# Filler transposes and matmuls on TensorE in the opening of a beacon-attention and maxout-FFN kernel

## The chip, the core and the metric

The kernel runs on one core of one Trainium2 chip. The metric is the device time of one execution in microseconds. The core has TensorE (PE in the profile; its weight loads are PEld), VectorE (DVE), ScalarE (ACT), GpSimd (POOL) and SyncE (SP), and 16 DMA engines. TensorE writes to banks of PSUM; the other engines read these and write SBUF.

## What is computed

Eight batches of eight heads of attention over 576 tokens and 16 beacon keys and values in front of them; the beacons are always visible, the rest is causal. The result is laid out as 4608 tokens of 512 features and goes through a feed-forward layer with the maximum of three products.

```python
k_all = concatenate([beacon_k, k], axis=2)     # 8 x 8 x 592 x 64
v_all = concatenate([beacon_v, v], axis=2)
scores = 1 / sqrt(64) * matmul(q, k_all.transpose(0, 1, 3, 2))
scores = where(causal, -1e9, scores)           # beacons are never masked
a = softmax(scores)
x = matmul(a, v_all).transpose(0, 2, 1, 3).reshape(4608, 512)
h = maximum(maximum(x @ w1, x @ w2), x @ w3)   # 512 -> 768
out = h @ w_out                                # 768 -> 512
```

## The kernel before

Everything on the matmul side is bf16. Heads are worked on in pairs, p from 0 to 31, four pairs a batch; two pairs make a quad. For a pair, q and k must first be turned so that the 64 features lie on partitions: the tile `qT` holds both heads of a pair on 2 x 64 partitions, `kT` the same with the 16 beacons in front. For the later batches that is a transposing DMA, for the first four batches TensorE transposes (L345, L360) with `ident` and an evacuation by VectorE or ScalarE.

The scores of a pair are made in four groups of (key tile, query range) pieces (L432, `emit_scores`): TensorE writes a group of both heads into a tile `sc` of two banks, of which there are two, and ScalarE takes the exponential of the whole group into `at_sb` (L451). Pieces on the diagonal are masked by VectorE (a product with `tri`, L468) or GpSimd (L470). `emit_pv` (L490) multiplies with ones and with v into the banks `pv0` and `pv1`, or into two `fps` banks; ScalarE inverts the sums (L534, L536) and VectorE multiplies (L546) into `xT`. FFN units (L565, L586, L605) use the `fps` banks.

The order of every engine's instructions is the order of the program's text (`tc.manual_schedule()`), so TensorE works strictly through its list; a wait there holds up all behind it. The opening, batch 0, has an order written out by hand in `start` (L711) and `first_steps` (L780). `T(p, h, pv)` (L752) there turns one half (288 tokens, h = 0 or 1) of pair p, by `turn_half` (L351): six transposes for q, an evacuation, six for k, an evacuation. The sources are the tiles `quad`, loaded by GpSimd's queue in `load_quad` (L206), q before k for each. With `pv` true the banks `pv0` and `pv1` are used, else two `fps` banks of bf16. `M` masks, `V` casts a tile of v, `P` is `emit_pv`, `F(n)` emits n FFN units, and `G(p)` loads a later pair with a gate: VectorE writes one element of the stage tile first, so that the load on SyncE's queue does not start ahead of VectorE's earlier work.

`keep_busy` (L407) multiplies the constant tile `busy` (ones, 128 x 320) with itself into the bank `pv1`; nobody reads the result. It is called with 12 at the start, and with 2 ahead of the second turn:

```python
    keep_busy(12)                        # L712
    ...
    turn_half(0, 0, False, by_act)       # L736
    turn_beacons(0, 1, bk16_0)
    cast_half(1, 0, by_dve)
    cast_half(1, 1, by_dve)
    keep_busy(2)                         # L740
    turn_half(1, 0, True)
```

Of the kernel before, what the change touches and what calls it, by code (L numbers as in the profile page):

```python
# [9 lines left out]
BF16 = mybir.dt.bfloat16  # L10
# [6 lines left out]
def kernel(  # L17
# [13 lines left out]
    nc = tc.nc  # L31
# [5 lines left out]
    d_model, d_ff = moe_w1.shape  # L37
# [12 lines left out]
    HALF = S // 2  # L50
# [70 lines left out]
    ffn_psum = ctx.enter_context(tc.tile_pool(name="ffn_psum", bufs=2, space=PSUM))  # L121
# [14 lines left out]
    busy = const.tile([128, 320], BF16, name="busy")  # L136
    nc.vector.memset(busy, 1.0)
    ident = const.tile([128, 128], BF16, name="ident")
# [15 lines left out]
    def pv_bank(i, shape, dtype):  # L154
        return pv_psum.tile(shape, dtype, name=f"pv{i}")
# [34 lines left out]
    def load_half(p, i, queue):  # L190
        st = half_pool.tile([QP, 2, HR, D], FP32, name=f"h32{i}")
        queue.dma_start(
            out=st.rearrange("p h r d -> p h (r d)"),
            in_=half_source(p // PPQ, 0, i, 2 * (p % PPQ), 2),
        )
        stage["half", p, i] = st

    def cast_half(p, i, cast):
        t16 = half_pool.tile([QP, 2, HR, D], BF16, name=f"h16{i}")
        cast(  # L200
            t16.rearrange("p h r d -> p (h r d)"),
            stage.pop(("half", p, i)).rearrange("p h r d -> p (h r d)"),
        )
        stage["half16", p, 0, i] = t16

    def load_quad(g, h):  # L206
        for i in range(2):
            t16 = const.tile([QP, 4, HR, D], BF16, name=f"quad{g}{h}{i}")
            nc.gpsimd.dma_start(  # L209
                out=t16.rearrange("p h r d -> p h (r d)"), in_=half_source(g, h, i, 0, 4)  # L210
            )
            for j in range(PPQ):
                stage["half16", PPQ * g + j, h, i] = t16[:, 2 * j : 2 * j + 2]
# [78 lines left out]
    def load_beacons(b0, b1, dst, queue=None):  # L292
        for b in range(b0, b1):
            (queue or nc.sync).dma_start(
                out=dst[Nb * (b - b0) : Nb * (b - b0 + 1)],
                in_=beacon_k[b].rearrange("h n d -> n h d"),
            )

    def turn_beacons(b0, b1, src):
        n = Nb * (b1 - b0)  # L300
        ps = sc_psum.tile([128, PPB, n], BF16, name="sc")
        for pi in range(PPB):
            nc.tensor.transpose(
                ps[:, pi],
                src[:, 2 * pi : 2 * pi + 2].rearrange("p h d -> p (h d)"),
                ident[0:n, 0:n],
            )
        if b0 == 0:
            by_act(kTs[0][:, 0:Nb], ps[:, 0, 0:Nb])
        by_act(bT[:, :, Nb * b0 : Nb * b1], ps)  # L310
# [37 lines left out]
                ident[0:QP, 0:QP],  # L348
            )

    def turn_half(p, h, pv, q_copy=None):  # L351
        for i in range(2):
            src = stage.pop(("half16", p, h, i))
            if pv:
                ps = pv_bank(i, [128, 1024], BF16)[:, 0:HALF]
            else:
                ps = ffn_psum.tile([128, HALF], BF16, name="fps")
            for r in range(HR):
                for e in range(2):
                    nc.tensor.transpose(  # L360
                        ps[64 * e : 64 * e + 64, r * QP : (r + 1) * QP],
                        src[:, e, r],
                        ident[0:QP, 0:QP],
                        tile_position=(0, 64 * e),
                    )
            x0 = i * Nb + HALF * h
            dst = (qTs, kTs)[i][p % NT][:, x0 : x0 + HALF]
            (q_copy if i == 0 and q_copy else by_dve)(
                dst.rearrange("d (p r) -> d p r", r=HR), ps.rearrange("d (r p) -> d p r", r=HR)
            )  # L370
# [7 lines left out]
    def place_beacons(p, copy):  # L378
        b, pi = divmod(p, PPB)
        copy(kTs[p % NT][:, 0:Nb], bT[:, pi, Nb * b : Nb * (b + 1)])  # L380
# [26 lines left out]
    def keep_busy(n, cols=320, ffn=False):  # L407
        ps = ffn_psum.tile([128, 512], FP32, name="fps") if ffn else pv_bank(1, [128, 512], FP32)
        for _ in range(n):
            nc.tensor.matmul(  # L410
                ps[:, 0:cols], busy[:, 0:128], busy[:, 0:cols], start=True, stop=True
            )
# [270 lines left out]
    def L(fn, *a):  # L683
        return lambda: fn(*a)
# [14 lines left out]
    def next_load(n=1):  # L699
        for _ in range(n):  # L700
            if loads:
                loads.pop(0)()
# [8 lines left out]
    def start():  # L711
        keep_busy(12)  # L712
        load_half(0, 0, nc.sync)
        load_half(0, 1, nc.scalar)
        load_half(1, 0, nc.sync)
        load_beacons(0, 1, bk32_0, nc.scalar)
        load_half(1, 1, nc.scalar)
        make_identity(nc, ident)
        nc.gpsimd.memset(tri, 1.0)
        nc.gpsimd.affine_select(  # L720
            out=tri,
            in_=tri,
            compare_op=ALU.is_ge,
            fill=0.0,
            base=0,
            pattern=[[1, 128]],
            channel_multiplier=-1,
        )
        load_quad(1, 0)
        load_quad(0, 1)  # L730
        load_quad(1, 1)
        next_load(3)
        cast_half(0, 0, by_dve)
        cast_half(0, 1, by_act)
        by_dve(bk16_0, bk32_0)
        turn_half(0, 0, False, by_act)  # L736
        turn_beacons(0, 1, bk16_0)
        cast_half(1, 0, by_dve)
        cast_half(1, 1, by_dve)
        keep_busy(2)  # L740
        turn_half(1, 0, True)
        place_beacons(1, by_dve)

# [5 lines left out]
    def steps(p):  # L749
        return [[0, 1], [2, 3]]  # L750

    def T(p, h, pv, q_copy=None):  # L752
        def run():
            turn_half(p, h, pv, q_copy)
            if h == 0:
                place_beacons(p, by_dve)

        return run

    def M(p, gi, dve=False):  # L760
        return L(emit_masks, p, gi, dve)
# [4 lines left out]
    def V(t):  # L766
        return L(cast_first_v, t)
# [7 lines left out]
    def F(n):  # L775
# [2 lines left out]
    cast_p = L(by_pool, bk16_1, bk32_1)  # L778

    first_steps = [  # L780
        ((0, 0), [T(2, 0, False)]),
        ((1, 0), [M(0, 0, True), T(3, 0, True), V(0), V(1)]),
        ((2, 0), [T(0, 1, False), V(2), L(load_w, 0, 0, d_ff)]),
        ((3, 0), [T(1, 1, True), M(1, 0, True), M(2, 0, True)]),
        ((0, 1), [M(0, 1)]),
        ((0, 2), [T(2, 1, False), M(3, 0, True), M(0, 2), V(3), V(4)]),
        ((0, 3), [M(0, 3, True), L(load_w, 1, 0, d_ff)]),
# [18 lines left out]
    for b in range(2, B):  # L806
        p = b * PPB
# [6 lines left out]
    for b in range(B_PE, B):  # L814
        p = b * PPB
# [8 lines left out]

    def emit_all():
        start()
        for group, fns in first_steps:
            if group:
# [104 lines left out]
```

## Time and profile before

| | |
|---|---|
| median of 5 runs | 304.03 us (303.51 to 304.90) |
| the profiled execution, its own time | 304.90 us |
| its span, first to last instruction | 303.2 us |
| TensorE busy | 286.6 us, 95% of the span |
| VectorE, ScalarE, GpSimd busy | 177.4, 144.9, 127.8 us |
| HBM read, written | 35.13, 14.22 MB |
| chain that ended last | PE 80%, DMA 5%, SyncE's queue 5%, DVE 3% |

The profiled execution is the slowest of the five shown, 0.87 us over the median; 1.7 us of it lie outside the span. "Busy" of TensorE counts from an instruction's start to a modelled end, and matmuls overlap, so it overstates the work. The page's slices divide the span in 40 parts of 7.58 us, with a digit for the busy share in tenths; PEclk is the clock that the throttle granted to TensorE. In rows of the timeline the first number is the start in us from the span's beginning, the second the length of the group, and the bracket gives the engine's idle time before it with what ended it. A form such as 96*64 96x96 is the rows and columns of the stationary operand, then partitions and columns of the moving one.

### The profile page before, as it was taken

How to read it: one execution, taken by the hardware profiler on the slowest of the kernel's cores; microseconds unless marked ns; L12 is line 12 of the kernel's file. 1: busy time of each engine (PE TensorE's matmuls, PEld its weight loads, DVE VectorE, ACT ScalarE, POOL GpSimd, SP SyncE). 2: the span in 40 equal slices, each digit the busy share in tenths (PEclk: the TensorE clock that was granted, in tenths of full speed). 3: DMA queues.
4: the chain of work that ended last, by engine and by line, in shares of the span. 5: the costliest groups of instructions: out<-in, count | busy, mean ns of one | idle time of the engine just before them, and what ended most of it. 6: DMA issues, size and time to landing. Idle time of an engine off the chain costs nothing.

```text
span 303.2 us, 8599 instructions
## 1 busy us (share of the span) xinstructions
PE 286.6 (95%) x3542; PEld 154.2 (51%) x3572; DVE 177.4 (59%) x357; ACT 144.9 (48%) x222; POOL 127.8 (42%) x253
## 2 busy tenths in 40 slices
PE   7898987999998999999999999999999999999994
PEld 3545653555444545454545687645454544444442
DVE  3753783655766575746674666466746675274372
ACT  3665475775565465635564556455645531401300
POOL 6170668466648674466445644562243210000000
PEclk9999999999999999999999999999999999999999
DMA  9995999999989999999979999994102001103003
GB/s 153 201 170 141 205 222 236 265 200 272 265 225 262 170 307 234 184 206 284 255 174 191 280 273 177 168 239 119 43 35 106 2 0 71 71 1 134 5 2 141
DMA packets 85320, 50.68 MB, mean 167 GB/s; under 512 B 64416, under 2 KB 80032, under 8 KB 85280
## 3 DMA queue, kind: packets, MB, share of 16 engines
q1 hardware_dynamic: 80672, 45.76, 66.9%
q0 software_dynamic: 4048, 4.03, 8.0%
q8 instruction: 28, 0.46, 0.7%
q10 hardware_dynamic: 560, 0.33, 0.5%
q14 instruction: 12, 0.10, 0.1%
HBM read 35.13 MB, written 14.22 MB: 163 GB/s over the span
## 4 chain that ended last, share of the span: by engine, by line
PE 80%; DMA 5%; SPq 5%; DVE 3%; POOL 2%; issue 2%; ACT 2%; POOLq 0%; DVEq 0%
PE fps L574 30%; PE sc L574 12%; PE pv L514 12%; PE fps L610 11%; PE sc L442 8%; PE sc L610 4%; SPq L245 3%; DMA quad<-in_k_dram 3%; DMA st<-in_k_dram 2%; PE sc L345 1%; ACT at_sb L451 1%; POOL quad L209 1%; SPq L180 1%; DVE y L618 1%; PE fps L514 1%
## 5 line engine op out<-in xcount | busy, mean ns | idle before, releaser
L451 ACT ACTIVATE at_sb<-sc 128x928 bf16<-128x928 f32 (+5 forms) x128 | 104.0, 861 | 89.7 <-PE sc L442 88.6
L574 PE MATMUL fps<-xT,w_sb 128*128 128x512 bf16 (+1 forms) x464 | 106.4, 356 | 2.4 <-issue 0.8
L470 POOL TENSOR_SCALAR_AFFINE_SELECT at_sb<-at_sb 128x256 bf16<-128x256 bf16 (+2 forms) x148 | 53.8, 383 | 103.0 <-ACT at_sb L451 102.8
L574 PEld LDWEIGHTS <-w_sb 128*128 128x128 bf16 x672 | 61.7, 97 | 65.5 <-issue 12.3
L584 DVE TENSOR_TENSOR hT<-hT,fps 128x512 bf16<-128x512 bf16 x70 | 47.9, 687 | 30.2 <-PE fps L574 29.7
L218 POOL CAST p<-st 96x768 bf16<-96x768 f32 x56 | 44.6, 822 | 0.5 <-DMA st<-in_k_dram 0.4
L574 PE MATMUL sc<-xT,w_sb 128*128 128x512 bf16 (+1 forms) x187 | 42.9, 356 | 0.1
L442 PE MATMUL sc<-qT,kT 64*128 64x288 bf16 (+5 forms) x400 | 38.1, 292 | 2.8 <-ACT at_sb L451 1.2
L610 PE MATMUL fps<-w_out_sb,hT 128*128 128x512 bf16 x143 | 34.6, 379 | 0.9 <-issue 0.6
L610 PEld LDWEIGHTS <-hT 128*128 128x128 bf16 x210 | 19.8, 98 | 24.1 <-DVE hT L584 2.1
L584 DVE TENSOR_TENSOR hT<-hT,sc 128x512 bf16<-128x512 bf16 x32 | 22.0, 688 | 16.3 <-PE sc L574 10.6
L618 DVE COPY y<-fps 128x512 f32<-128x512 f32 x25 | 17.3, 691 | 22.7 <-PE fps L610 22.7
L514 PE MATMUL pv<-at_sb,v_sb 128*32 128x288 bf16 (+5 forms) x1376 | 29.6, 233 | 0.0
L442 PEld LDWEIGHTS <-kT 64*128 64x128 bf16 x400 | 14.9, 97 | 28.1 <-issue 23.1
L582 DVE CAST hT<-fps 128x512 bf16<-128x512 f32 x32 | 22.0, 690 | 12.1 <-PE fps L574 12.1
L546 DVE TENSOR_TENSOR xT<-pv,recip 128x288 bf16<-128x288 f32 (+2 forms) x93 | 27.2, 348 | 2.6 <-ACT recip L536 2.6
L514 PEld LDWEIGHTS <-v_sb 128*32 128x32 bf16 (+1 forms) x1408 | 25.0, 98 | 2.7 <-issue 0.6
L514 PE MATMUL pv<-at_sb,ones 128*32 128x288 bf16 (+4 forms) x500 | 18.6, 263 | 1.1 <-POOL at_sb L470 0.9
L261 POOL CAST v_sb<-st 128x1536 bf16<-128x1536 f32 (+2 forms) x21 | 18.4, 893 | 0.6 <-DMA st<-in_v_dram 0.6
L534 ACT ACTIVATE lnd<-pv 128x288 f32<-128x288 f32 x31 | 12.9, 416 | 8.2 <-PE pv L514 8.1
L514 PEld LDWEIGHTS <-ones 128*32 128x32 bf16 (+2 forms) x512 | 11.2, 97 | 9.6 <-issue 6.6
L582 ACT CAST hT<-sc 128x512 bf16<-128x512 f32 x6 | 3.5, 586 | 23.7 <-PE sc L574 23.7
(70 smaller groups left out, 165.1 us busy)
## 6 DMA issues: line engine op xcount, KB each, us to landing
out_dram<-y SPq DMA_DIRECT2D x35, 256.0 KB, 3.1
st<-in_q_dram SPq DMA_DIRECT2D x28, 288.0 KB, 5.3
st<-in_k_dram SPq DMA_DIRECT2D x28, 288.0 KB, 5.7
st<-in_v_dram SPq DMA_DIRECT2D x24, 256.0 KB, 5.9
w_sb<-in_moe_w_dram POOLq DMA_DIRECT2D x6, 384.0 KB, 6.7
q_dram<-p SPq DMA_DIRECT2D x16, 144.0 KB, 2.4
k_dram<-p SPq DMA_DIRECT2D x16, 144.0 KB, 2.7
st<-in_v_dram SPq DMA_DIRECT2D x8, 224.0 KB, 6.2
```

Source lines behind the costliest of these rows:

```text
L218: cast(t16.rearrange("p r h d -> p h r d"), st[0:QP, i * NQ2 : (i + 1) * NQ2].rearrange("p (h r d) -> p h r d", h=2, r=QR),)
L261: cast(v_sb[0:n, t:t1].rearrange("p t h d -> p (t h d)"), st[0:n, (t - t_lo) * H * D : (t1 - t_lo) * H * D],)
L442: nc.tensor.matmul(ps[:, e, off : off + q1 - q0], kT[hs, 128 * t : 128 * t + 128], qT[hs, q0:q1], start=True, stop=True, tile_position=(64 ...
L451: nc.scalar.activation(out=both_heads(p, gi), in_=ps[:, :, 0 : g_width(p, gi)], func=AF.Exp, scale=scale)
L470: nc.gpsimd.affine_select(out=view, in_=view, compare_op=ALU.is_ge, fill=0.0, base=x0, pattern=[[0, 2], [1, hi - lo]], channel_multiplier=-1,)
L514: nc.tensor.matmul(ps[bank][32 * j : 32 * j + 32, lo + q0 - qa : lo + qb - qa], lhsT, at_view(PPQ * quad + j // 2, t, j % 2, q0, qb), star ...
L546: nc.vector.tensor_mul(xT[:, 2 * g + part - 1, c0 + ca : c0 + cb], ps[bank][:, lo : lo + cb - ca], recip[:, ca:cb],)
L574: nc.tensor.matmul(ps[:, o0 : o0 + n], w_in[i][:, ct, 128 * ft : 128 * (ft + 1)], xT[:, ct, x0 : x0 + n], start=(ct == 0), stop=(ct == n_c ...
L582: (by_act if alone[0] else by_dve)(h, ps)
L584: nc.vector.tensor_max(h, h, ps)
L610: nc.tensor.matmul(ps, hT[:, ft, 128 * tt : 128 * (tt + 1)], w_out_sb[:, ft, :], start=(ft == 0), stop=(ft == n_ft - 1),)
L618: nc.vector.tensor_copy(y, ps)
```

## The change

`turn_half` gets an argument `idle`. Ahead of the k transposes of a turn it now puts that many transposes of `busy` by `ident`, 128 x 128 each, into columns 512 to 1023 of the bank that the k transposes are about to write in columns 0 to 287; nobody reads these columns. Four turns of `first_steps` get six each. The `fps` tile of a turn is now 1024 columns of bf16, a whole bank. After the very first turn `keep_busy(3)` is added. TensorE's list grows by 27 weight loads and 27 matmuls or transposes; the lists of the other engines and the DMAs stay as they were.

```diff
+    def fill(ps, n):
+        for i in range(n):
+            x0 = 512 + 128 * (i % 4)
+            nc.tensor.transpose(ps[:, x0 : x0 + 128], busy[:, 0:128], ident)
+
-    def turn_half(p, h, pv, q_copy=None):
+    def turn_half(p, h, pv, q_copy=None, idle=0):
         for i in range(2):
             src = stage.pop(("half16", p, h, i))
             if pv:
-                ps = pv_bank(i, [128, 1024], BF16)[:, 0:HALF]
+                bank = pv_bank(i, [128, 1024], BF16)
             else:
-                ps = ffn_psum.tile([128, HALF], BF16, name="fps")
+                bank = ffn_psum.tile([128, 1024], BF16, name="fps")
+            ps = bank[:, 0:HALF]
+
+            fill(bank, idle if i == 1 else 0)
             for r in range(HR):
...
         turn_half(0, 0, False, by_act)
+        keep_busy(3)
         turn_beacons(0, 1, bk16_0)
...
-    def T(p, h, pv, q_copy=None):
+    def T(p, h, pv, q_copy=None, idle=0):
         def run():
-            turn_half(p, h, pv, q_copy)
+            turn_half(p, h, pv, q_copy, idle)
...
-        ((0, 0), [T(2, 0, False)]),
-        ((1, 0), [M(0, 0, True), T(3, 0, True), V(0), V(1)]),
-        ((2, 0), [T(0, 1, False), V(2), L(load_w, 0, 0, d_ff)]),
-        ((3, 0), [T(1, 1, True), M(1, 0, True), M(2, 0, True)]),
+        ((0, 0), [T(2, 0, False, None, 6)]),
+        ((1, 0), [M(0, 0, True), T(3, 0, True, None, 6), V(0), V(1)]),
+        ((2, 0), [T(0, 1, False, None, 6), V(2), L(load_w, 0, 0, d_ff)]),
+        ((3, 0), [T(1, 1, True, None, 6), M(1, 0, True), M(2, 0, True)]),
```

## The prediction

> **What bounds the kernel now.** I read the slice rows of the page first, then the chain of waits over the first 40 us, then TensorE's timeline of the opening, and last ScalarE's.
>
> ```profile
> PE   7898987999998999999999999999999999999994
> PEclk9999999999999999999999999999999999999999
> DMA  9995999999989999999979999994102001103003
> ```
>
> A slice is 7.58 us. From the eighth slice on TensorE is full to the end but for one digit, so whatever is won or lost before about 50 us is carried to the end unless something else paces the stretch between. PEclk says full clock everywhere, even in the first slices, and that is where this page misleads: the matmuls themselves say otherwise.
>
> ```profile
> 1.32 3.38 PE L410 MATMUL pv<-busy 128*128 128x320 bf16 x12 [1.32 <-DVE busy L137]
> ...
> 8.37 0.45 PE L360 MATMUL fps<-ident,quad 96*64 96x96 bf16 x6
> 9.11 0.45 PE L360 MATMUL fps<-ident,quad 96*64 96x96 bf16 x6 [0.29 <-DMA quad<-in_k_dram]
> 9.49 0.61 PE L442 MATMUL sc<-qT,kT 64*128 64x288 bf16 x6
> 10.03 0.69 PE L360 MATMUL pv<-ident,quad 96*64 96x96 bf16 x12
> 10.66 0.61 PE L442 MATMUL sc<-qT,kT 64*128 64x288 bf16 x6
> 11.19 0.45 PE L360 MATMUL fps<-ident,quad 96*64 96x96 bf16 x6
> 12.01 0.45 PE L360 MATMUL fps<-ident,quad 96*64 96x96 bf16 x6 [0.37 <-DMA quad<-in_k_dram]
> 12.40 0.61 PE L442 MATMUL sc<-qT,kT 64*128 64x288 bf16 x6
> 12.93 0.69 PE L360 MATMUL pv<-ident,quad 96*64 96x96 bf16 x12
> ...
> 25.95 1.74 PE L593 MATMUL fps<-xT,w_sb 128*128 128x256 bf16 x8
> ...
> 28.56 1.05 PE L593 MATMUL fps<-xT,w_sb 128*128 128x256 bf16 x8
> ```
>
> The columns are start, length, engine, line, instruction, count, and the idle time before with what ended it. The last two lines are the same eight matmuls: 1.74 us at 25.95, 1.05 us at 28.56. With the 0.28 us tail of the last one taken off, the seven gaps are 0.21 us and 0.11 us. The twelve dummies at the top start 0.267 us apart, 0.83 ns a column; the later rate is half that. So **the gate is shut from the first instruction to about 27.4 us** (the starts of single instructions change pace at 27.4, where the trace's clock record also begins; the page takes the time before it for full). Even transposes obey it: the 96-column ones of L360 take 281 ns, those of L345 at 35 us take 206 ns.
>
> Before about 15 us TensorE works in its fixed order behind the quarter loads:
>
> ```profile
> 5.36 9.73 DMA quad<-in_k_dram
> 15.09 0.04 issue
> 15.13 0.45 PE fps L360 x6
> 15.58 0.94 PE sc L442 x6
> 16.52 2.00 PE pv L514 x37
> ```
>
> This is the chain of waits. After 15.1 it is TensorE almost without a break (pv, sc, fps, pv, fps) to 27.7, interrupted by one ScalarE exponential at 22.5, then by the one at 28.05, and at 29.4 it goes through the gated pair loads into SyncE's queue and the transfers, until a cast at 50.3. Beside it runs ScalarE:
>
> ```profile
> 13.05 4.50 ACT L451 ACTIVATE at_sb<-sc 128x1024 bf16<-128x1024 f32 x5 [0.72 <-PE sc L442]
> 18.98 0.78 ACT L451 ACTIVATE at_sb<-sc 128x736 bf16<-128x736 f32 x1 [1.43 <-PE sc L442]
> ```
>
> Five exponentials back to back from 13.05 to 17.55. With two score buffers, the scores of the fifth of these wait for the third exponential. A delay ahead of 13.05 therefore reaches the first big pv stretch at 16.45 through ScalarE, however early the last load lands.
>
> **The change, part by part.** Nothing is removed or moved, no DMA is added, and every queue but TensorE's keeps its order. The waits on a bank's earlier user pass from the k transposes to the fills ahead of them; a fill waits for a bank, never for the load behind it. What is added is 3 matmuls of 320 columns and 24 transposes of 128 columns.
>
> *The three dummies after the first turn.* The first turn issues its last transpose at 5.22, and the beacon transposes wait for a VectorE cast until 6.37 (0.86 us idle in the row of L303). Three times 0.267 us is 0.80 us: 5.35 to 6.15. Cost nothing, covered by that cast; if the cast were earlier, up to 0.8 us.
>
> *The fills at the shut clock.* Six times 128 columns at 0.83 ns is 0.64 us each. The trace has no such transpose. Below: with the clock open, half, 0.32 us. Above: if the 128-column weight loads did not overlap, another 0.10 us each (the weight loads of L410 last 102 to 152 ns, yet its matmuls start exactly 320 columns apart, so they do overlap), 1.26 us. I take 0.64, by the L410 row.
> - T(2,0): q transposes leave the array at 8.62, fill to about 9.29, k at 9.33 instead of 9.11, for which the load (landed 9.07) was the limit: +0.22.
> - T(3,0): its k half is already there and no idle lies between; the whole 0.64: +0.86 so far.
> - T(0,1): q ends at 12.28 instead of 11.42, fill to 12.92, k at 12.97 instead of 12.01: +0.96. The load's wait of 0.37 has covered part.
> - T(1,1): no wait again, +0.64: +1.60 on the scores of (0,1), from 13.56 to 15.15.
>
> Then ScalarE: its exponential of (3,0) begins at 14.0, and (0,1) at 15.7 rather than 14.07, with a hole of 0.7 in what was a full row. The fifth group's scores follow the third exponential, and pv goes from 16.45 to about 18.05. The quad wait at 15.1 hides 0.3 us of TensorE's delay, but not of ScalarE's. **Sum if the gate stays shut: +1.6 us at 16.45.** From there the chain is TensorE itself to 27.7, so nothing absorbs it; the gated loads start 1.6 later, and so does the DMA stretch. Lower bound +0.3 (only TensorE's own delay counts, and most of the rest goes under ScalarE's and the loads' gaps), upper +2.2 (some of the weight loads showing).
>
> *The gate itself.* How much of a stretch does the array stream, at 0.83 ns a column, pairs on two halves counted once? From 8.37 to 15.51: ten half-turns of 0.24, three score groups of 0.43, one of 0.41, one of 0.31, together 4.4 of 7.14 us, 0.62. The stretch before the one that opened (17.2 to 20.6) comes to 0.67 and did not open it; that of 24.0 to 27.4, dense pv and FFN matmuls, comes to 0.96 and did. With four fills the stretch becomes 7.0 of about 8.7 us, 0.80: between the two, in a region that the trace has not tried.
>
> [...] By the row alone, with transposes counted as streaming, 0.80 might do. [...] That transposes run faster at an open gate (281 against 206 ns) shows that they obey it, not that they feed it; no row here shows the latter. [...]
>
> **The rivals.**
> *A, gate stays shut through the fills (my forecast).* +1.6: 304.90 becomes 306.5 on the profiled execution, which was the slowest of the five, 0.87 above the median. On the median 304.03 + 1.6 = **305.6**. Own range 304.8 to 306.3. [...] Against: every stretch of 8 to 15 us is fuller than before.
> *B, the fills open the gate, between 10 and 17 us.* TensorE's row from 15.5 to 27.7 holds some 10.4 us of streaming; half of it would go, 5.2. But ScalarE follows: from 17.55 to the end of the two exponentials at 25.49 it has 5.4 us of work that needs each other in turn, so I estimate the first gated load 1.4 us earlier and the second, behind the exponential of 28.05, 2.6 us earlier, after the roughly 0.95 that the first three fills cost. DMA then paces to 50 us; its busy share falls to 0.46 between 25 and 30 us (1.04 in the five before), and that slack is what an earlier gated load can use. I take 2.0: 302.0, with 300.8 to 303.2. It decides from the point where a fill-filled window passes the gate's unknown limit, between 0.67 and 0.96.
> *C, the gate opens late*, about 20 us, half way to today's 27.4, as the three real matmul groups come nearer together. Then half of B's saving pays for A's cost: 304.0, within 0.9.
> [...]
>
> **How the numbers follow.** About 0.3% (0.9 us) is what a measurement of this kernel can tell from no change. A 0.53, B 0.39, C 0.08. A's low end within 0.9 takes 0.03, B's 0.02, C 0.05 with the rest split: faster 0.38, same 0.10, slower 0.52. The range of 301.3 to 306.3 leaves out B's best and A's worst, about 0.2.
>
> **What would show it.** If A is right, the fills are 107 ns apart, the eight matmuls of the first FFN unit still take about 1.7 us, pv's first stretch begins near 18, and the clock record begins at 27 us or later. If B is right, that record begins before 17, pv's first stretch takes about 1.1 us instead of 2.0, and the second gated pair load leaves SyncE before 28 us instead of 29.4. Fills under 0.4 us a set while the clock is shut, or a pv stretch at 16.5 in spite of them, would make the step through ScalarE wrong. Windows that differ from run to run in where they fall would show as a wider scatter than 303.5 to 304.9.

## The result and the profile after

| | before | changed |
|---|---|---|
| median of all executions | 303.94 us (47) | 303.33 us (26) |
| spread | 302.52 to 305.77 | 300.79 to 311.31 |
| ratio, with its 95% interval | | 0.9952 (0.9933 to 0.9971) |
| profiled execution, own time and span | 304.90, 303.2 us | 300.99, 299.3 us |

The ratio leaves out executions more than 1.5% above their kernel's fastest, which drops seven of the changed kernel's and none of the kernel before, so it flatters a kernel whose times spread (below it drops two of six in experiment 3, six of twelve in experiment 4, five of twelve in the second set of the changed kernel, and none of the best version). Over all executions the changed kernel's median is 0.6 us lower and its mean 0.1 us (303.94, before 304.05). A second set of twelve executions of the changed kernel, told below, gave a median of 305.20 against 304.44 before, ratio 0.9988 (0.9959 to 1.0018), and means of 304.76 against 304.58. So the median gains a little in one set and loses in the other, and on average the change is worth next to nothing. The cause of that is the finding of this case: **the changed kernel has several times, not one**, because the granted clock takes a different course in different executions (its mean lies between 0.961 and 1.000 in the 27 listed).

The profiled execution is one of the good ones. Its slices on the page:

```profile
PE   7788878999999999999999999999999999999994
PEclk9999999999999999999999999999999999999999
DMA  8999999999999998999889999983111002103003
```

They look like those before, so the difference lies in the timeline of TensorE (start, length, group, idle before it):

```profile
4.63 0.74 PE L368 MATMUL fps<-ident,h 96*64 96x96 bf16 x12
5.30 0.65 PE L418 MATMUL pv<-busy 128*128 128x320 bf16 x3
6.25 0.25 PE L303 MATMUL sc<-ident,bk 16*128 16x16 bf16 x4 [0.30 <-DVE bk L743]
...
7.97 0.51 PE L354 MATMUL fps<-ident,busy 128*128 128x128 bf16 x6
9.48 0.32 PE L368 MATMUL fps<-ident,quad 96*64 96x96 bf16 x6 [0.99 <-DMA quad<-in_k_dram]
...
16.44 0.97 PE L522 MATMUL pv<-at_sb,v_sb 128*32 128x288 bf16 x32
...
24.00 0.83 PE L601 MATMUL fps<-xT,w_sb 128*128 128x256 bf16 x6 [0.70 <-DMA w_sb<-in_moe_w_dram]
...
25.70 1.05 PE L601 MATMUL fps<-xT,w_sb 128*128 128x256 bf16 x8
```

Of the kernel before, the v part of the first pv stretch:

```profile
17.11 1.40 PE L514 MATMUL pv<-at_sb,v_sb 128*32 128x288 bf16 x32
```

The three dummies take 0.65 us with their tail, less than the 0.80 forecast without one, because the gate opens while they run: the trace's clock record begins at 5.47 us, against 27.41 before. A set of q transposes takes 0.32 us instead of 0.45, six fills 0.51 with their tail, and the v part of the first pv stretch 0.97 instead of 1.40. The chain of waits now has, up to 24 us, transfers of v and of the FFN weights; from 15 us on TensorE stood there before:

```profile
3.98 11.32 DMA st<-in_v_dram
...
16.48 7.48 DMA w_sb<-in_moe_w_dram
23.95 0.05 issue
24.00 0.83 PE fps L601 x6
24.83 0.34 PE sc L450 x4
...
26.55 0.31 SPq L180
```

The gated pair loads leave earlier, the first at 22.99 instead of 25.25 and the second at 26.55 instead of 29.41. SyncE's timeline before, and after:

```profile
25.25 0.31 SPq L180 DMA_DIRECT2D st<-in_q_dram  x1
...
29.41 0.31 SPq L180 DMA_DIRECT2D st<-in_q_dram  x1
```

```profile
22.99 0.31 SPq L180 DMA_DIRECT2D st<-in_q_dram  x1
...
26.55 0.31 SPq L180 DMA_DIRECT2D st<-in_q_dram  x1
```

After that both executions run the same course some 3 to 4 us apart. The start is now short enough that the first FFN unit waits 0.70 us for its weights, which had 3.85 us to spare before (landed at 22.10, used at 25.95).

### The profile page after: what moved, and what is told of

Same layout as the page of the kernel before. It is cut to its first block, busy times and chain, and to the rows that moved or that the text cites. A ratio compares the mean times of both kernels' runs of the same rounds, so it can differ in the third digit from the quotient of the medians.

```text
span 299.3 us, 8653 instructions
## 1 busy us (share of the span) xinstructions
PE 282.0 (94%) x3569; PEld 152.9 (51%) x3599; DVE 177.0 (59%) x357; ACT 144.8 (48%) x222; POOL 127.5 (43%) x253
## 4 chain that ended last, share of the span: by engine, by line
PE 73%; DMA 11%; SPq 6%; DVE 3%; issue 2%; ACT 1%; POOL 1%; POOLq 0%; DVEq 0%
PE fps L582 28%; PE sc L582 12%; PE fps L618 11%; PE pv L522 10%; PE sc L450 7%; PE sc L618 4%; DMA st<-in_v_dram 4%; DMA st<-in_k_dram 4%; SPq L245 4%; DMA w_sb<-in_moe_w_dram 2%; SPq L180 1%; PE sc L345 1%; DMA h<-in_q_dram 1%; ACT at_sb L459 1%; DVE kT L392 1%
## 5 line engine op out<-in xcount | busy, mean ns | idle before, releaser
L450 PE MATMUL sc<-qT,kT 64*128 64x288 bf16 (+5 forms) x400 | 35.7, 277 | 3.0 <-ACT at_sb L459 1.4
L522 PE MATMUL pv<-at_sb,v_sb 128*32 128x288 bf16 (+5 forms) x1376 | 28.7, 229 | 0.0
L450 PEld LDWEIGHTS <-kT 64*128 64x128 bf16 x400 | 14.3, 94 | 27.0 <-issue 22.8
L522 PEld LDWEIGHTS <-v_sb 128*32 128x32 bf16 (+1 forms) x1408 | 24.4, 96 | 1.9 <-issue 0.6
L522 PE MATMUL pv<-at_sb,ones 128*32 128x288 bf16 (+4 forms) x500 | 17.9, 256 | 0.3
```

The lines of the kernel that those rows point to most:

```text
L450: nc.tensor.matmul(ps[:, e, off : off + q1 - q0], kT[hs, 128 * t : 128 * t + 128], qT[hs, q0:q1], start=True, stop=True, tile_position=(64 ...
L522: nc.tensor.matmul(ps[bank][32 * j : 32 * j + 32, lo + q0 - qa : lo + qb - qa], lhsT, at_view(PPQ * quad + j // 2, t, j % 2, q0, qb), star ...
```

## The experiments

Two quantities are used throughout. *The gate's course*: the trace of a profiled execution records when the granted clock changed, between 1.0, called open, and 0.5, called shut; ahead of the first record the pace of the matmuls tells it. For every other execution only the mean granted clock over its span is listed, which counts the time before the first record as full (1.000 for the kernel before, whose record begins at 27.41 us). So 0.996 to 1.000 (all twelve executions of the kernel without dummies, experiment 8) is read as a gate that opened once, whenever; one that opens early, shuts for 20.5 us and opens again should give about 0.966, an estimate from half clock for 20.5 us of 303 (the profiled execution of the fills as matmuls, shut for 23.9 us, has 0.961). What is said below of executions without a trace is read from this mean. *The streamed share of a window*: columns times 0.83 ns while shut and half of it while open (dummies of 320 columns start 0.267 us apart at the shut clock, matmuls of 256 columns 0.11 us at the open one, both in the kernel before), overlaps counted once, worked out from the starts and shapes in the traces. A window, here and in the prediction, is a stretch of 3.41 us, laid from the first change of the clock record. The length is the spacing of these changes: in the run with fills alone (below) they lie at 4.99, 8.41 and 28.89 us, one and six times 3.41 apart; in the traces of the fills as matmuls and of the fills only in waits the gaps are one and seven, and two and five; in those of the kernel before and of the changed kernel the one rise and the fall at the end lie 276.48 and 293.55 us apart, 81 and 86 times 3.413. The traces show when the clock changed and not how that is decided: that it goes by the streamed share of such a window is a reading, and the experiments give the shares that it rests on.

**1. Dummies alone.**

```diff
-            fill(bank, idle if i == 1 else 0)
```

> Changed kernel without its 24 fill transposes; keep_busy(3) stays. Theory W (the gate opens when one window of about 3.4 us, whose place differs from execution to execution, is at least 0.9 streamed; the dense first 5 us hold such a window in about half of the executions once the three dummies fill the hole after the first turn; the fills then keep later windows full enough that the gate doesn't shut again): the gate opens near 5 us as often as in the changed kernel but shuts again in the load waits from 7 to 15 us, so few executions near 301 us, times of 303 to 304.5, median 303.7. Rival D (the three dummies do it all, the fills only cost): same spread as the changed kernel with its low end near 301 or lower, and no executions above 305.5, median 302.3. Rival F (the fills open the gate): like the kernel before, 304.0.

Measured: 304.41 us (303.49 to 305.65, 12 executions), ratio 0.9999 (0.9978 to 1.0019). Ten of twelve have a mean clock of 0.963 to 0.972: the gate opened early and shut again. The dummies are free, as the prediction had it, and with them the gate opened early more often (34 of 77 in the kernel before, experiment 8); by themselves they are also worth nothing. The expected median was too low by 0.7, and the opening far more frequent than the half expected. The 0.9 of theory W is near the 0.91 of the changed kernel's window from 2.06 to 5.47, after which its gate opened; windows of 0.81 and 0.83 did it too (below).

**2. Fills alone.**

```diff
-        keep_busy(3)
```

> Changed kernel without keep_busy(3), fills as they are. Theory W: windows of at least 0.9 exist for places over only 0.9 us out of 3.41, so about a quarter of the executions near 301 us, and the others near 305.6 because the fills run at the shut clock (+1.6 on the kernel before); median 304.8. Rival D: no execution near 301, all near 305.5. Rival F: same as the changed kernel, about half near 301.

Measured: 306.52 us (304.97 to 311.09, 12), ratio 1.005 (1.0026 to 1.0074). A quarter of the executions was expected near 301; none is. Five have a mean clock of 0.960 to 0.966: they opened early, and all five lost the gate in spite of the fills. Seven have 0.998 to 1.000 and lie at 305.73 or above, so the fills did not open a shut gate in time to gain. This is the predicted case A, and its price: 1.9 us on the medians (306.52 and 304.64), and 2.0 for the seven alone (median 306.57, beside 304.55 for executions of the kernel before with such a clock). The windows of its profiled execution, one of the five, show the gate open for one window, then shut until 28.9 (busy TensorE time with instructions, then PEclk, DMA share and GB/s):

```profile
5.00:8.40 3.40, 2.34 (x44) 1.00 1.35 187
8.40:11.80 3.40, 3.19 (x40) 0.50 1.41 186
11.80:15.20 3.40, 3.40 (x42) 0.50 1.34 215
15.20:28.80 13.60, 12.40 (x193) 0.50 0.77 137
28.90:32.00 3.10, 3.10 (x64) 1.00 0.59 171
```

The window that lost it, 4.99 to 8.41, was streamed 0.36: the hole that the three dummies fill in the changed kernel stands in it (in the changed kernel's trace the window after the opening, 5.47 to 8.89, holds 0.45). So in these two traces the gate was kept where the dummies fill the hole and lost where they don't.

The same execution shows the fills at the shut clock, and ScalarE behind them (two lines of TensorE's timeline, then two of ScalarE's):

```profile
10.36 0.82 PE L354 MATMUL pv<-ident,busy 128*128 128x128 bf16 x6
...
18.49 0.74 PE L522 MATMUL pv<-at_sb,ones 128*32 128x288 bf16 x12
```

```profile
14.20 1.02 ACT L459 ACTIVATE at_sb<-sc 128x1024 bf16<-128x1024 f32 x1 [1.03 <-PE sc L450]
16.24 3.35 ACT L459 ACTIVATE at_sb<-sc 128x992 bf16<-128x992 f32 x4 [1.02 <-PE sc L450]
```

ScalarE has holes of 1.0 us ahead of its exponentials, and pv starts at 18.49 instead of 16.45. (The time of this one execution, 311, also holds a pause of 4.3 us at 90 us, outside the opening. Single times of 309 to 311 in other runs are not explained by their clock alone; whether they hold such a pause is not known.)

**3. Fills as matmuls.** The 24 fills go as matmuls of the same 128 columns into the bank `pv1`.

```diff
+            if i == 1 and idle:
+                keep_busy(idle, 128)
...
-            fill(bank, idle if i == 1 else 0)
```

> Changed kernel, but the 24 fills are matmuls of busy by busy of the same 128 columns, into the bank pv1. Theory that transposes count for the gate as matmuls do: same spread as the changed kernel, about half of the executions near 301, median 303 within 0.8. Theory that a transpose does not count as busy: with real matmuls the gate opens in the fill-filled stretch from 8 to 14 us also where the opening missed it, and stays open; most executions between 300.5 and 302.5.

Measured: 302.58 us (300.44 to 306.62, 6), ratio 0.9899 (0.9865 to 0.9932). Four of six lie between 300.4 and 303.2, one at 306.44 (clock 0.961) and one at 306.62 (0.998). These last two speak against the second expectation: real matmuls did not open the gate in the stretch from 8 to 14 us either. In the profiled one the gate opened at 4.86, shut at 8.28 and stayed shut until 32.17, with streamed shares of 0.61 and 0.68 in the windows of the fills; in the fills alone, with transposes, they were 0.68 and 0.72. Six executions do not tell whether matmuls hold the gate a little better than transposes.

**4. The opening as transposes.**

```diff
-        keep_busy(12)
...
         make_identity(nc, ident)
+        turn_dummies(30)
...
+    def turn_dummies(n):
+        ps = pv_bank(1, [128, 1024], BF16)
+        for i in range(n):
+            x0 = 128 * (i % 8)
+            nc.tensor.transpose(ps[:, x0 : x0 + 128], busy[:, 0:128], ident)
```

> Changed kernel, but the twelve opening dummies of 320 columns are 30 transposes of 128 columns, as many columns in all. If transposes feed the gate: about half of the executions near 301, as in the changed kernel, median 303. If they don't: no window before 8 us holds more than 0.4 of matmul streaming, so the gate never opens early: nearly all executions at 305 or above, median 305.6.

Measured: 304.44 us (299.98 to 309.92, 12), ratio 0.9924 (0.9891 to 0.9957). The gate opened early in at least eleven of twelve: two were lost for six windows (clock 0.963), six for three or four (0.977 to 0.982), two for one or two (0.991, 0.993), one is the profiled one, and one ran in 299.98. Its timeline:

```profile
1.42 3.36 PE L428 MATMUL pv<-ident,busy 128*128 128x128 bf16 x30 [1.42 <-DVE kT L149]
4.71 0.69 PE L368 MATMUL fps<-ident,h 96*64 96x96 bf16 x12
5.33 0.98 PE L418 MATMUL pv<-busy 128*128 128x320 bf16 x3
```

The clock record begins at 6.45. The window from 3.03 to 6.45 was streamed 0.83, but only the three dummies of 0.80 us in it are matmuls, 0.23. In the run with dummies alone, windows with 0.61 and 0.69 in matmuls (3.69 to 7.11 and 0.28 to 3.69) left the gate shut, so the share of matmuls alone does not tell these windows apart, and the share with transposes does. **The transposes of this kernel feed the gate**, as far as these two traces show it. The median was expected at 303; it is higher because the gate was lost for some windows in ten executions. Why that is more than in the changed kernel's first set is not settled.

**5 to 7. More dummies, and fills where TensorE waits.** In the windows traced up to here, shut ones of up to 0.77 stayed shut and those from 0.83 opened the gate; open ones of 0.43 and more kept it, those of 0.36 and 0.42 lost it. Three kernels were built on these shares, each with the next diff on top of the one before it, and the changed kernel went again beside them.

```diff
-        keep_busy(3)
+        keep_busy(6)
...
-        keep_busy(2)
+        keep_busy(3)
```

> Changed kernel with six dummies after the first turn instead of three, and three instead of two ahead of the second turn; fills as in the change. Theory W2 (a window of 3.41 us opens the gate when the array streams about 0.8 of it, whether by matmuls or by transposes, and the gate stays open while a window holds over about 0.43; where the windows lie is drawn anew for each execution): every place of the windows now finds a full one before 7.7 us, and the window after it is fuller by 0.15, so nearly all executions keep the gate open: median 301.3, few above 303. Rival (the opening of the gate depends on something else than the fill of a window, and a part of the executions always misses): the same spread as the changed kernel, 300.8 to 307, with a median near 303.3.

Measured: 302.66 us (301.48 to 308.64, 12), ratio 0.9945 (0.9918 to 0.9971). Six of twelve lie under 302.5, against three of twelve in the changed kernel beside it. Better, but the median missed the expected 301.3 by 1.4: three were lost for long (0.972 to 0.977) and three for one or two windows. Opening earlier was not enough here.

```diff
-        ((0, 0), [T(2, 0, False, None, 6)]),
-        ((1, 0), [M(0, 0, True), T(3, 0, True, None, 6), V(0), V(1)]),
+        ((0, 0), [T(2, 0, False, None, 16)]),
+        ((1, 0), [M(0, 0, True), T(3, 0, True, None, 2), V(0), V(1)]),
...
-        ((3, 0), [T(1, 1, True, None, 6), M(1, 0, True), M(2, 0, True)]),
+        ((3, 0), [T(1, 1, True, None, 2), M(1, 0, True), M(2, 0, True)]),
...
-        ((0, 2), [T(2, 1, False), M(3, 0, True), M(0, 2), V(3), V(4)]),
+        ((0, 2), [T(2, 1, False, None, 12), M(3, 0, True), M(0, 2), V(3), V(4)]),
```

> As the kernel with more dummies, but the fills moved to where TensorE idles behind a load when the gate is open: 16 in the turn of (2,0), 2 in (3,0), 6 in (0,1), 2 in (1,1) and 12 in (2,1). Theory W2: windows from 8 to 16 us hold over 0.5, the gate stays open in nearly all executions, and ScalarE's holes of 0.24 us before two exponentials go: median 300.8. Rival (the fills' places don't matter): as the kernel with more dummies, within 0.3. If most executions lie above 303, the hold level is higher than read.

Measured: 301.22 us (300.29 to 303.94, 6), ratio 0.9901 (0.9869 to 0.9934). The median is 0.4 above the expected one. None lost the gate for long; one has 0.987.

```diff
-        ((1, 0), [M(0, 0, True), T(3, 0, True, None, 2), V(0), V(1)]),
+        ((1, 0), [M(0, 0, True), T(3, 0, True, None, 0), V(0), V(1)]),
...
-        ((3, 0), [T(1, 1, True, None, 2), M(1, 0, True), M(2, 0, True)]),
+        ((3, 0), [T(1, 1, True, None, 0), M(1, 0, True), M(2, 0, True)]),
```

> As the one before, without any fill in the turns (3,0) and (1,1), where no load is waited for. Theory W2: a window between 9.5 and 13 us now holds 0.40 to 0.45 and some executions lose the gate there: a median between 300.6 and 302, with some executions at 303 to 304.5. If the fills in these two turns only cost, all executions lie at 300.5 to 301.5.

Measured: 302.34 us (301.06 to 306.27, 12), ratio 0.9933 (0.9907 to 0.9959), 0.3 above the expected range of the median. Three are lost for long, as the theory had it and the rival had not. The profiled one is among them and shows where (PEclk is the fourth figure; open, shut, open):

```profile
5.70:12.50 6.80, 5.76 (x97) 1.00 1.39 191
12.60:29.50 16.90, 16.12 (x230) 0.50 0.86 166
29.60:33.00 3.40, 3.40 (x67) 1.00 0.35 90
```

The last window before the loss, 9.10 to 12.51, was streamed 0.41. The two turns' fills, which have no idle time of TensorE under them, stand in this window; without them three of twelve executions lose the gate for long, with them none of fourteen (this run's neighbour above and its second set, below).

> The changed kernel once more, beside these three on one chip. Theory W2: the same mixture as before, about half of the executions within 302.5, a quarter at 303 to 305.2 that lost the gate for some windows, a quarter over 305.5 that opened it late; median 302 to 304. Rival (the two groups come from the chip that was drawn): one group alone.

Measured: 305.20 us (300.78 to 310.77, 12). Three held the gate (300.78 to 302.49), four lost it for three or four windows (303.35 to 305.48), five for five windows or more (305.19 to 310.77). The expected median, 302 to 304, was missed: the mixture was a worse one this time, with none opened late. All twelve ran on one chip, so the chip does not make the groups; that it shifts their shares is possible and was not tried.

**8. The best version again, and no dummies at all.**

> The kernel with more dummies and its fills in the waits once more, for a second draw of its few executions. Theory W2: nearly all executions keep the gate open from before 8 us; median 301.2 within 0.6, at least three quarters under 302.5. If its lead was a lucky draw of window places: a median over 302.5.

Measured: 301.55 us (300.77 to 303.85, 8), ratio 0.9911 (0.9881 to 0.9941). The median is as expected; the three quarters under 302.5 are not reached (five of eight). The version with more dummies and with its fills in the waits holds its lead over the kernel before in both draws, with 14 executions between 300.29 and 303.94, and over the changed kernel in the one set where both ran (301.22 and 305.20). (The fills as matmuls have as good a ratio, 0.9899, but it leaves out the two of six above 306; their mean over all six is 303.35, beside 301.54 and 301.95 here.) Its timeline shows fills where a load was awaited:

```profile
8.23 1.07 PE L354 MATMUL fps<-ident,busy 128*128 128x128 bf16 x16
9.23 0.32 PE L368 MATMUL fps<-ident,quad 96*64 96x96 bf16 x6
...
14.46 0.84 PE L354 MATMUL fps<-ident,busy 128*128 128x128 bf16 x12
15.24 0.32 PE L368 MATMUL fps<-ident,quad 96*64 96x96 bf16 x6
```

The wait for the k quarter (0.99 us before 9.48 in the changed kernel) is filled to the end, and so is the one before 15.06 (0.71 us there).

```diff
-        keep_busy(12)
...
-        keep_busy(2)
```

> The kernel before without any dummy (neither the twelve at the start nor the two ahead of the second turn). Theory W2: the gate never opens early, and as the kernel before shuts it again after one window wherever it opens it early, nothing is lost: 304.5 within 0.5 of the kernel before on the same chip. Rival (the single open window near 5 us in a part of the executions before was worth something): 305.2 or more.

This is the kernel before without its own fourteen dummies. Measured: 304.59 us (303.85 to 305.67, 12), ratio 1.000 (0.9979 to 1.0021), all twelve with a clock of 0.996 or more, read as never opened early. In the three comparisons, 34 of 77 executions of the kernel before have 0.957 to 0.966 and a median of 304.70; the other 43 have 304.55. By the mean clock, the early opening that the kernel before had in these 34, four of nine, lasted about one window; it was worth nothing. No trace caught one of them.

**What followed which share**, over all traces, as streamed shares of single windows:

| gate | window | what followed |
|---|---|---|
| shut | at most 0.77 (dummies alone, 3.69 to 7.11) | stayed shut |
| shut | 0.81 to 0.96 (the lowest: more dummies, 0.69 to 4.10) | opened |
| open | 0.36, 0.41, 0.42 (fills alone, fills only in waits, fills as matmuls) | shut |
| open | from 0.41 (the changed kernel again, 6.15 to 9.56) and 0.42 (more dummies, 14.34 to 17.76) upward | stayed open |

At 0.41 and 0.42 both outcomes occur, and one record missing in a trace could move a share by more than that difference (a matmul of 288 columns is 0.12 us at the open clock, 0.035 of a window; an estimate). The profile's own busy time does not tell the outcomes apart: in the dummies alone TensorE counts as busy for 3.40 of 3.42 us from 4.99 to 8.41, with the gate shut. Whether a share that weighs rows or weight loads would do it better was not tried.

A check from the traces that stay shut in the opening: laid over their starts, about half of all places of the windows (0.47) give the kernel before a window of 0.8 or more in its first 10 us, 0.71 give the dummies alone one, and none the kernel without dummies. That is an estimate, with every place taken as equally likely; the executions that opened early are 34 of 77, 10 of 12 and none of 12.

## Why the prediction was wrong

The forecast was 305.6, slower by 1.6 us because the gate stays shut through the fills. Measured is 303.33, faster by 0.6 in this set. That the number lies inside the stated range, 301.3 to 306.3, is no merit of the mechanism: it is the middle of a mixture that the prediction did not have. Point by point:

- *What bounds the opening* was right: the gate shut, loads to 15 us, TensorE and ScalarE to 29, gated loads after that. Where the gate held, the gain went the way described, through the gated loads: 2.26 us earlier for the first (estimated 1.4) and 2.86 for the second (2.6).
- *"The gate is shut from the first instruction to about 27.4 us"* was right for that execution and was taken for all. It was one of two kinds; 34 of 77 open for one window near 5 us. One profile cannot show what differs from one execution to the next. The last of the signs named, a wider scatter if the windows fall differently from run to run, is the one that came: 300.79 to 311.31.
- *The three dummies: "Cost nothing"* was right for their time (ratio 0.9999 alone), and **here is the step that failed**: they were priced as time under a VectorE cast, and their effect on the gate was put at nothing, with the gate taken as shut until the fills come. The share was worked out for the stretch from 8.4 us on alone, where the fills stand and after it. The first five microseconds, dense with twelve dummies and twelve transposes, were never summed; there the share already reaches 0.9 for some places of the windows, and the three dummies widen the places at which it passes 0.8 (from 0.47 to 0.71 of them, by the estimate above). Alone they raised the early openings from 34 of 77 to 10 of 12; with the fills behind them, only three of 27 executions in the first set and none of twelve in the second have the clock and the time of a gate that opened late. Neither part gains by itself (304.41 with the dummies alone, 306.52 with the fills alone); the times near 301 come where the start opens the gate and dummies and fills then hold it.
- *Where the gate opens.* "0.80: between the two, in a region that the trace has not tried" was a fair reading, since tried: a window of 0.77 stayed shut, one of 0.81 opened. The 0.80 itself was too high: the two windows of the fills at the shut clock held 0.68 and 0.72 in the run with fills alone, and the gate stayed shut, as case A had it. (The shut stretch of 0.67, called the one before the opening, is two windows before it; the one between holds 0.54.) But the question for the fills was another one. They hold open what the start has opened, and for that windows of 0.43 and more at the open clock were enough in every trace. That the gate was kept at shares so far below those that opened it (0.81 and more) was missing from the sum.
- *Whether transposes feed the gate.* "No row here shows the latter", the prediction says, and its choice of case A took them not to. That was the author's assumption, and no run shows it. The opening as transposes speaks against it for the transposes of this kernel: 0.23 by matmuls alone, 0.83 with transposes, and the gate opened. Taking them to count would not have repaired the forecast, since the fills did not open the gate in these runs either way.
- *Case A's price*, +1.6, was right in mechanism: pv at 18.49 (18.05 forecast), through holes in ScalarE's row (1.0 us ahead of four exponentials in turn, where one of 0.7 was forecast), and 1.9 to 2.0 us at the end. But it needs a gate that is shut through the fills. In the first set of the changed kernel that holds throughout for the three executions at 306.5 to 306.8, the ones with a clock of 0.999.
- *Case B's price*, 302.0, was close: in the first set the eight executions that keep the gate take 300.99 to 303.10, with a median of 301.65. That is in part luck, since its way there was wrong: the gate opens at 5 to 6 us in the two traces, not "between 10 and 17 us", and by the dense start, not by the fills. Its 10.4 us of streaming from 15.5 to 27.7 us come to 8.7 by the measure of the windows, and the first pv stretch takes 1.4 us (15.99 to 17.41), not the 1.1 named as a sign.
- *The chances* put case A over B by treating them as alternatives of which one is true. Both happen, in shares. The small gain of the first set is their mixture; of the 27 executions whose clock is listed the first set holds eleven with a clock of at least 0.996, of which eight took 303.1 or less, beside sixteen that lost the gate for one window or more.

## What to carry to other kernels

Read from traces of the kernel at hand when the granted clock changes and how far apart, and work out the streamed share of TensorE over every place of such a window in the opening, not over one stretch. Here, with 3.41 us, the gate opened after shut windows of 0.81 and more, was lost in open ones of 0.36 to 0.42 and kept in all of 0.43 and more, so the start had to be dense wherever the windows fell, and no window behind it thin; whether these shares hold for another kernel no run shows. Put filler where a load is awaited, sized to that wait at the open clock (medians of 301.22 and 301.55 us here, 305.20 for the changed kernel beside the first); filler while the gate is shut cost 2.0 us here. And when a change acts on something that differs from one execution to the next, read the distribution and the clock of every execution ahead of any median, and ask of a ratio which executions it leaves out.

## What the runs showed that was not expected

- The mean clock of the page counts the time before its first record as full: the profiled execution before ran 27.4 us at half speed under a printed 1.000.
- The gate opened after shut windows of 0.81 to 0.96 and none up to 0.77, was lost in open ones of 0.36, 0.41 and 0.42 and kept in some of 0.41 and 0.42 and in all above, with windows of 3.41 us. Their place against the program's start differs between executions: 5.47 and 6.15 us for the first opening in two executions of the changed kernel (over the traces with an early one: 4.10, 4.86, 4.99, 5.47, 5.68, 6.07, 6.15, 6.45 and 6.69 us).
- One open window near 5 us changes nothing in the time (304.70 and 304.55). That what runs there waits for loads anyway is the likely reason; no run tests it.
